# Two orders on VectorE in a gated attention and MLP kernel: A12 - S2 behind the forms of T2, and A22's scaling between two parts of A12's

## The chip, the cores and the metric

The kernel runs on one core of a Trainium2 chip. The metric is the device time of one execution in microseconds; 731.65 is the median of the three runs before the change. A core has a matrix engine (TensorE, PE in the profile), a vector engine (VectorE, DVE), an engine for activations and copies (ScalarE, ACT), GpSimd (POOL), and SyncE (SP), which here only issues transfers. Each engine has an instruction stream of its own and works it off in order; semaphores join them. The DMA engines move data between the core's memory and HBM.

## The reference

x is 2048 tokens by 1024. Two branches work on it and a gate per token mixes them:

```python
    x = A_x
    g = _sigmoid((x * gate_w).sum(-1, keepdims=True))
    a = _A_ref(x, A_wqkv, A_wo)
    b = _B_ref(x, B_w_gate, B_w_up, B_w_down)
    return g * a + (1 - g) * b
```

Branch A is attention with 32 heads of 32, in which a token sees 8 keys, itself and every second one before it (offsets 0, 2, ... 14); its output is multiplied by wo (1024 by 1024). Branch B is an MLP: h = gelu(x @ w_gate) * (x @ w_up) with 3584 columns, then h @ w_down. Both last products end in the same 2048 by 1024 result.

## The kernel before, in words

**Stages.** First come the projections (q, k, v, and 14 pairs of gate and up), with the attention worked off on DVE beside them. `h` and the attention's output are stored to HBM (`h_d`, `o_d`). Then comes the down stage. It treats both last products as one: the row of left operands is [h, attention output], the right operand is w_down above wo. It is done in two passes of 1024 tokens: `down(0)`, then `down(1)`.

**One pass.** The left operand is cut into four blocks A11, A12, A21, A22 (a half of the tokens by a half of the inner rows), the right one into R11, R12, R21, R22. The product is made with Winograd's form of Strassen's scheme: seven block products instead of eight, on sums of blocks. On the left these are S1 = A21 + A22 (`S` in the code), S3 = A11 - A21 (`AD`), S2 = A22 - S3 (written over A21), and S4 = A12 - S2 (written over A12). On the right they are T1 to T4, made earlier, stored in HBM and loaded back. The products are A11 R11, A12 R21, S1 T1, S2 T2, A12 R22 (where A12 holds S4 by then), S3 T3 and A22 T4. Three of them in pass 0, and four in pass 1, are cut once more in the same way (`level2`): that needs second-level sums, four for the left block (`forms_L`, line 985) and four for the right one (`forms_R`, line 993), all on DVE. `level2` is 126 matmuls of 256 columns (line 1024); a plain block product (`mm`, line 1049) is 72 matmuls of 512 columns.

**Scaling.** h has to be multiplied by 1 - g. For the last 2 of the 14 pairs that is done before h is stored. For the first 12 (`NE_` = 12) it is done in the loaded blocks, in place, by `scale_task` (line 906), four row groups to an instruction, so a block takes three. The sums of blocks (`comb_task`, line 913) take five instructions for a block of 18 row groups.

**Buffers.** Ten buffers of one block each hold everything, by the table `plan`. In pass 0 A12 is in buffer 2, A22 in 3, A21 in 6 and S in 8; R21 and then L6 (the left forms for S2) are in 7; T1 and then R6 (the right forms for T2) are in 1; T2 is in 9; A11, L5 and R22 follow each other in 4, and R11, R5 and T4 in 5. A load into a buffer waits until its last reader is done.

**The order around the change.** The order on each engine is that of the program text; nothing reorders it. Near the end of the projections `pre_down_2` issues the load of A22 (its first 12 row groups) and queues the scalings as tasks that run once the last projection is done. A12's and A21's first 11 row groups were loaded before; `pre_down_3` loads their twelfth, with R21 and the attention's rows, on SyncE's queue in this order: R21, A12's row and attention rows, A21's row and attention rows, A22's attention rows. The loads of T1 and T2 stand behind them. When the tasks are done, `down(0)` runs on DVE: the scaling of A21's last row group, S, AD, the forms of S and T1 (L5, R5), S2 over A21, the forms of S2 (L6), then the lines that the change touches, then `joins` (line 1013), which adds a part of the second-level product to the banks that ScalarE then copies out (line 1106). PE in the meantime runs A11 R11, A12 R21 and `level2` for S1 T1 and for S2 T2; the latter begins with two products that take S2 and T2 as they are, and its third product takes the first forms. In pass 1 (`last`) the lines of the change don't apply: there the five pieces of A12 - S2 stand behind the forms of T2.

```python
            run(forms_L(B["L6"], S2))
            rest = comb_task(A12, A12, S2, ALU.subtract)
            if not last:
                take(rest, 3)
            run(forms_R(B["R6"], B["T2"]), rest)
```

`take(rest, 3)` issues three of the five pieces of A12 - S2; `run` issues all that is left of its generators, one after the other.

Of the kernel before, what the change touches and what calls it, by code (L numbers as in the profile page):

```python
# [68 lines left out]
def kernel(  # L69
# [54 lines left out]
    NE_ = NPAIR - 2  # L124
# [10 lines left out]
    with tc.manual_schedule(engines={mybir.EngineType.PE, mybir.EngineType.DVE, mybir.EngineType.Activation,  # L135
# [296 lines left out]
        def bg(gen, prio, wake):  # L432
            t = Task(gen, prio, wake)
            tasks.append(t)
            tasks.sort(key=lambda t_: t_.prio)
            return t
# [288 lines left out]
        def pv_all():  # L725
# [48 lines left out]
            while now[0] < n - 6:  # L774
                yield None
            pre_down_2(0)

        def late_forms():
# [31 lines left out]
        def load_A(b, s, half, c, i0, i1, with_o, eng=nc.sync):  # L810
            for e, (a, z) in enumerate(((i0, min(i1, NE_)), (max(i0, NE_), i1))):
                if z > a:
                    src = h_d[s][e][:, :, c * SC:(c + 1) * SC].rearrange("p (i two) s -> p i two s", two=2)
                    eng.dma_start(out=b[:, a:z, :], in_=src[:, a - e * NE_:z - e * NE_, half, :])
            if with_o:
                nc.sync.dma_start(out=b[:, NH_:NK, :], in_=o_d[s][c][:, half * 4:half * 4 + 4, :])
# [81 lines left out]
        def Bs(s):  # L898
            return {k: bufs[v] for k, v in plan[s].items()}

        def scale_task(b, s, c, ia, ib):
            t0 = s * SUP + c * SC
            om = omgrep[:, t0:t0 + SC].rearrange("p (o s) -> p o s", o=1)
            for i0 in range(ia, ib, 4):
                i1 = min(i0 + 4, ib)
                TT(out=b[:, i0:i1, :], in0=b[:, i0:i1, :], in1=om.to_broadcast([P, i1 - i0, SC]), op=ALU.mult)
                yield 0.05 + 0.273 * (i1 - i0)

        def comb_task(o_, a, b, op, step=4):
            for i0 in range(0, NK, step):  # L910
                i1 = min(NK, i0 + step)
                f = lambda t_: flat(t_[:, i0:i1, :])
                TT(out=f(o_), in0=f(a), in1=f(b), op=op)  # L913
                yield 0.05 + 0.273 * (i1 - i0)

        def run(*gens):
            for g in gens:
                for _ in g:
                    pass
# [5 lines left out]
        def take(g, k):  # L925
            for _ in range(k):
                if next(g, None) is None:
                    break
# [14 lines left out]
        def pre_down_2(s):  # L943
            pd["end"] = True
            load_A(Bs(s)["A22"], s, 1, 1, 0, NE_, False)
            for k, c in (("A12", 0), ("A22", 1)):
                bg(scale_task(Bs(s)[k], s, c, 0, NE_), 7, n)
            if now[0] >= NX0 + 3:
                pre_down_3(s)

        def pre_down_3(s):
            loads(s, "R21")
            load_A(Bs(s)["A12"], s, 1, 0, KX, NE_, True)
            load_A(Bs(s)["A21"], s, 0, 1, KX, NE_, True)
            load_A(Bs(s)["A22"], s, 1, 1, 0, 0, True)
# [24 lines left out]
        def forms_L(f, b):  # L980
            f = quads(f)
            q = lambda kh, h: quarter(b, kh, h)
            for o_, a, b_, op in ((f[:, 0], q(0, 1), q(1, 1), ALU.add), (f[:, 1], f[:, 0], q(0, 0), ALU.subtract),
                                  (f[:, 2], q(0, 0), q(0, 1), ALU.subtract), (f[:, 3], q(1, 0), f[:, 1], ALU.subtract)):
                TT(out=o_, in0=a, in1=b_, op=op)  # L985
                yield 1.3

        def forms_R(f, b):
            f = quads(f)
            q = lambda kh, h: quarter(b, kh, h)  # L990
            for o_, a, b_, op in ((f[:, 0], q(0, 1), q(0, 0), ALU.subtract), (f[:, 1], q(1, 1), f[:, 0], ALU.subtract),
                                  (q(0, 1), q(1, 1), q(0, 1), ALU.subtract), (f[:, 2], q(1, 0), f[:, 1], ALU.subtract)):
                TT(out=o_, in0=a, in1=b_, op=op)  # L993
                yield 1.3

        def woven(*gens):
            for cs in zip(*gens):
                yield from cs
# [41 lines left out]
        def down(s):  # L1040
            B = Bs(s)
            last = s == 1
# [18 lines left out]
            A11, A12, A21, A22, S, AD = (B[k] for k in ("A11", "A12", "A21", "A22", "S", "AD"))  # L1061
            XP = [bank(XT[j]) for j in range(4)]
            VP = [bank(VT[j]) for j in range(4)]
            if last:
                run(scale_task(A12, s, 0, 0, NE_))
                level2(XT, A11, B["R11"], B["L1"], B["R1"])
                rest = comb_task(AD, A11, A21, ALU.subtract)
# [28 lines left out]
            level2(VT, S, B["T1"], B["L5"], B["R5"])  # L1096
            run(forms_L(B["L6"], S2))
            rest = comb_task(A12, A12, S2, ALU.subtract)
            if not last:
                take(rest, 3)  # L1100
            run(forms_R(B["R6"], B["T2"]), rest)

            def mid6():
# [13 lines left out]
            rest = woven(forms_L(B["L7"], AD), forms_R(B["R7"], B["T3"]))  # L1117
# [24 lines left out]
        n = len(units)  # L1142
# [4 lines left out]
        def run_last(b):  # L1147
            now[0] = b
            prv = units[b - 1]
            for t_ in [t_ for t_ in tasks if t_.wake < b]:  # L1150
                t_.finish()
            prv.p73()
            first = down(0)
            next(first)
            prv.p4()
            loads(0, "T1", "T2")
            for t_ in list(tasks):
                t_.finish()
            run(first)
            run(down(1))  # L1160
# [60 lines left out]
```

## Time and profile before

| | |
|---|---|
| median of 3 runs | 731.65 us (731.50 to 731.73) |
| the profiled execution | 731.21 us, span 729.4 us |
| PE busy | 714.7 us (98%), mean granted clock 0.995 |
| DVE busy | 655.1 us (90%) |
| ACT busy | 317.2 us (43%) |
| POOL busy | 114.7 us (16%) |
| PE matmuls of `level2` (line 1024) | 882, 100.3 us, mean 277 ns |
| PE matmuls of `mm` (line 1049) | 492, 109.3 us, mean 379 ns |
| DVE sums of blocks (line 913) | 40, 41.9 us, mean 1110 ns |
| pass 0 in the trace | from 512.5 us (first matmul of line 1049) to about 623 |
| pass 1 in the trace | from about 623 us to 729 |

How to read it: the span is the time from the first to the last instruction in the profile; the device time of that execution is 1.8 us longer. Matmuls overlap in the array, so the mean length of one is longer than the distance from one to the next. Engines carry line numbers of the kernel before; a line of the trace's timeline gives start, length, engine, line, operation, operands, how many instructions were merged into it, and in brackets how long the engine was idle before and what it waited for. A row of the windows gives the stretch, its length, the busy time with the number of instructions of PE, the weight loads, DVE, ACT and POOL, then the granted TensorE clock, the busy share of the DMA engines and the GB/s.

### The profile page before, as it was taken

What the parts mean: (1) busy time and instruction counts of PE and PEld (TensorE: products, weight loads), DVE (VectorE), ACT (ScalarE), POOL (GpSimd) and SP (SyncE); (2) the same over time, 40 slices, a digit from 0 to 9 for tenths busy, and PEclk for the clock granted to TensorE, in tenths of its full rate; (3) what the DMA queues carried; (4) which work ended last, traced back from release to release, by engine and by line L of the source; (5) the groups of instructions that cost most, each with busy time, mean ns of one, the idle gap of its engine ahead of it and who ended that gap; (6) DMA issues with size and microseconds to landing.
All of it is one profiled execution on the core that took longest, in us unless ns stands there. A gap on an engine that the chain in (4) does not pass through costs nothing. (4 is left out here: it accounts for less than half of the span.)

```text
span 729.4 us, 10330 instructions
## 1 busy us (share of the span) xinstructions
PE 714.7 (98%) x3883; PEld 393.0 (54%) x3945; DVE 655.1 (90%) x703; ACT 317.2 (43%) x570; POOL 114.7 (16%) x212
## 2 busy tenths in 40 slices
PE   8999999999999999999999999999998999999998
PEld 4466666655544444444444444444457666758573
DVE  3699999999999999999999999999599698799944
ACT  4554445444557665555555555555131211232210
POOL 1233445143201210000010000001110011110001
PEclk9999999999999999999999999999999899999999
DMA  9967644287274834443363836563975766965501
GB/s 279 279 184 224 206 140 154 78 283 268 98 213 136 284 118 146 137 154 113 120 203 115 276 118 224 133 234 100 364 315 179 271 229 211 380 276 199 199 22 58
DMA packets 112626, 140.78 MB, mean 193 GB/s; under 512 B 18832, under 2 KB 94768, under 8 KB 111552
## 3 DMA queue, kind: packets, MB, share of 16 engines
q1 hardware_dynamic: 98368, 98.38, 42.0%
q0 software_dynamic: 13920, 41.21, 15.7%
q8 instruction: 31, 0.51, 0.3%
q10 hardware_dynamic: 288, 0.52, 0.3%
q14 instruction: 19, 0.16, 0.1%
HBM read 98.01 MB, written 39.99 MB: 189 GB/s over the span
## 5 line engine op out<-in xcount | busy, mean ns | idle before, releaser
L364 PE MATMUL banks<-arena 128*128 128x512 bf16 x2136 | 472.1, 380 | 4.1 <-DVE arena L401 0.7
L364 PEld LDWEIGHTS <-arena 128*128 128x128 bf16 x2184 | 240.2, 111 | 235.6 <-issue 7.0
L1049 PE MATMUL banks<-arena 128*128 128x512 bf16 x492 | 109.3, 379 | 1.0 <-ACT arena L1106 0.4
L401 DVE TENSOR_TENSOR arena<-banks,arena 128x1024 bf16<-128x1024 f32 x78 | 95.2, 1220 | 13.0 <-PE banks L364 7.6
L1024 PE MATMUL banks<-arena 128*128 128x256 bf16 x882 | 100.3, 277 | 3.7 <-DVE arena L993 3.7
L387 ACT COPY arena<-banks 128x512 f32<-128x512 f32 x78 | 45.7, 586 | 130.8 <-PE banks L364 130.8
L1024 PEld LDWEIGHTS <-arena 128*128 128x128 bf16 x882 | 87.3, 99 | 16.8 <-issue 4.2
L1049 PEld LDWEIGHTS <-arena 128*128 128x128 bf16 x504 | 49.2, 98 | 59.1 <-issue 0.6
L372 ACT CAST arena<-banks 128x512 bf16<-128x512 f32 x102 | 59.6, 584 | 42.4 <-PE banks L364 42.4
L743 DVE TENSOR_TENSOR arena<-arena 128x2048 bf16<-128x2048 bf16 x64 | 77.0, 1219 | 0.5
L750 DVE TENSOR_TENSOR arena<-arena 128x2048 bf16<-128x2048 bf16 (+2 forms) x96 | 73.8, 775 | 1.0
L596 DVE TENSOR_TENSOR arena<-arena 128x2048 bf16<-128x2048 bf16 x64 | 74.6, 1218 | 0.1
L394 ACT COPY banks<-banks 128x512 f32<-128x512 f32 x78 | 44.5, 570 | 21.9 <-PE banks L364 20.1
L258 POOL DMA_DIRECT2D h_d<-arena x28 | 15.1, 541 | 242.0 <-DVE arena L252 213.1
L382 ACT COPY banks<-banks 128x512 f32<-128x512 f32 x78 | 45.0, 576 | 13.6 <-PE banks L364 12.1
L1054 POOL DMA_DIRECT2D out_dram<-arena x28 | 15.2, 541 | 179.8 <-DVE arena L1058 130.0
L913 DVE TENSOR_TENSOR arena<-arena 128x2048 bf16<-128x2048 bf16 (+1 forms) x40 | 41.9, 1110 | 0.0
L1029 ACT COPY banks<-banks 128x256 f32<-128x256 f32 x42 | 14.9, 356 | 57.2 <-PE banks L1024 57.0
L321 DVE TENSOR_TENSOR arena<-arena 128x1024 bf16<-128x1024 bf16 x60 | 38.6, 685 | 0.5
L252 DVE TENSOR_TENSOR arena<-arena 128x2048 bf16<-128x2048 bf16 x28 | 34.0, 1216 | 5.5 <-ACT arena L372 4.1
L370 ACT ACTIVATE arena<-banks 128x512 bf16<-128x512 f32 x54 | 32.2, 597 | 15.4 <-PE banks L364 15.4
L985 DVE TENSOR_TENSOR arena<-arena 128x2304 bf16<-128x2304 bf16 x28 | 37.5, 1352 | 0.5
(85 smaller groups left out, 434.1 us busy)
## 6 DMA issues: line engine op xcount, KB each, us to landing
arena<-t_d SPq DMA_DIRECT2D x8, 2304.0 KB, 12.5
h_d<-arena POOLq DMA_DIRECT2D x28, 512.0 KB, 3.6
arena<-in_B_w_down_dram SPq DMA_DIRECT2D x6, 1792.0 KB, 14.5
t_d<-arena POOLq DMA_DIRECT2D x36, 256.0 KB, 4.1
arena<-h_d SPq DMA_DIRECT2D x6, 1536.0 KB, 11.0
arena<-in_B_w_gate_dram SPq DMA_DIRECT2D x15, 512.0 KB, 5.2
arena<-in_B_w_up_dram SPq DMA_DIRECT2D x15, 512.0 KB, 4.6
arena<-in_B_w_down_dram SPq DMA_DIRECT2D x28, 256.0 KB, 7.0
```

The source lines that it names most:

```text
L364: self.pe = nc.tensor.matmul(ps, lhsT=self.L[form](kt), rhs=rhs[:, kt, :], start=(start and kt == 0), stop=(kt == HK - 1), skip_group_chec ...
L372: nc.scalar.copy(out=o_, in_=i_)
L382: nc.scalar.copy(out=self.Y, in_=self.X)
L387: nc.scalar.copy(out=self.p5s, in_=self.V)
L394: nc.scalar.copy(out=self.Z, in_=self.Y)
L401: TT(out=self.T[:, :, c2s], in0=pair, in1=self.p5s.rearrange("p (o n) -> p o n", o=1).to_broadcast([P, 2, SC]), op=ALU.add)
L596: TT(out=dst, in0=q.rearrange("p (o s) -> p o s", o=1).to_broadcast([P, NWIN, AC]), in1=_win_ap(k, [[-DIL, NWIN], [1, AC]]), op=ALU.mult)
L743: TT(out=prod2[(t // 2) % 2][:, t % 2], in0=ab, in1=_win_ap(v[:, t, HALO:HALO + AC], [[SJ, NJ], [-DIL, NWIN], [1, SJ]]), op=ALU.mult)
L750: TT(out=out_, in0=h(0), in1=h(1), op=ALU.add)
L913: TT(out=f(o_), in0=f(a), in1=f(b), op=op)
L1024: nc.tensor.matmul(c(i, h, j), lhsT=l[:, kt, j * P:(j + 1) * P], rhs=r[:, kt, :], start=False, stop=(kt == KH - 1), skip_group_check=True)
L1049: nc.tensor.matmul(ps, lhsT=L[:, i, j * P:(j + 1) * P], rhs=R[:, i, :], start=(start and q == 0), stop=(q == NK - 1), skip_group_check=not ...
```

## The change

Two edits. In `pre_down_2` the scaling of A12 is cut into two tasks, and A22's task is put between them: before, DVE scales A12's three pieces and then A22's three; after, A12's first two, A22's three, and then A12's third, which holds the twelfth row group. In `down`, pass 0 no longer issues three pieces of A12 - S2 ahead of the forms of T2: all five come behind them, as in pass 1.

```diff
         def pre_down_2(s):
             pd["end"] = True
             load_A(Bs(s)["A22"], s, 1, 1, 0, NE_, False)
-            for k, c in (("A12", 0), ("A22", 1)):
-                bg(scale_task(Bs(s)[k], s, c, 0, NE_), 7, n)
+            for k, c, ia, ib in (("A12", 0, 0, 8), ("A22", 1, 0, NE_), ("A12", 0, 8, NE_)):
+                bg(scale_task(Bs(s)[k], s, c, ia, ib), 7, n)
             if now[0] >= NX0 + 3:
                 pre_down_3(s)
...
             run(forms_L(B["L6"], S2))
             rest = comb_task(A12, A12, S2, ALU.subtract)
-            if not last:
-                take(rest, 3)
             run(forms_R(B["R6"], B["T2"]), rest)
```

## The prediction

> **What bounds the kernel now.** The page's first part comes first: TensorE (PE) is busy 98% of the span and VectorE (DVE) 90%, so only places where PE stands still can be worth time. The chain of waits goes back from the end to 656.13 us alone, too late for this change. So I took the list of waits, then PE's and DVE's timelines around its two rows:
>
> ```profile
> DVE arena L906 <- DMA arena<-h_d: 3.0, 1, 3.0
> PE banks L1024 <- DVE arena L993: 3.7, 1, 3.7
> ```
>
> (Columns: total us, times, longest.) DVE once waits 3.0 us for a load in the scaling; PE once waits 3.7 us for DVE's forms of T2. PE's timeline (start, length, instruction) around that wait, and two lines of the second pass:
>
> ```profile
> 544.42 18.00 PE L1024 MATMUL banks<-arena 128*128 128x256 bf16 x162
> 566.08 12.64 PE L1024 MATMUL banks<-arena 128*128 128x256 bf16 x90 [3.67 <-DVE arena L993]
> 578.56 15.70 PE L1049 MATMUL banks<-arena 128*128 128x512 bf16 x70
> ...
> 652.69 27.88 PE L1024 MATMUL banks<-arena 128*128 128x256 bf16 x252
> 680.95 15.70 PE L1049 MATMUL banks<-arena 128*128 128x512 bf16 x70 [0.39 <-ACT arena L1106]
> ```
>
> The same 252 matmuls (two level2 calls) take 34.14 us start to start in pass 0 (578.56 - 544.42) and 28.26 in pass 1. The wait is only 3.67 of it: 90 matmuls after it take 12.48 us, against 9.95 at pass 1's rate (27.88/252 = 110.6 ns). The windows give the reason in the column PEclk, TensorE's granted clock:
>
> ```profile
> 544.40:562.40 18.00, 18.00 (x163) 15.81 (x162) 17.80 (x16) 5.11 (x13) 0.54 (x1) 1.00 0.36 113
> 566.10:568.00 1.90, 1.90 (x10) 1.31 (x10) 1.86 (x2) 0.00 (x0) 0.00 (x0) 0.50 1.00 427
> 568.00:570.00 2.00, 2.00 (x11) 1.40 (x10) 2.00 (x3) 0.37 (x1) 0.00 (x0) 0.50 0.44 184
> 572.00:573.00 1.00, 1.00 (x12) 0.89 (x10) 0.98 (x2) 0.38 (x2) 0.00 (x0) 1.00 0.00 0
> 680.50:681.00 0.50, 0.12 (x2) 0.05 (x1) 0.50 (x2) 0.50 (x2) 0.00 (x0) 1.00 0.00 0
> ```
>
> The clock is half after the 3.67 us wait, full again by 572, and stays full over pass 1's 0.39 us stall. DVE up to the wait:
>
> ```profile
> 520.01 2.36 DVE L906 TENSOR_TENSOR arena<-arena,omgrep 128x2048 bf16<-128x2048 bf16 x2
> 525.37 4.97 DVE L906 TENSOR_TENSOR arena<-arena,omgrep 128x2048 bf16<-128x2048 bf16 x5 [3.00 <-DMA arena<-h_d]
> 530.25 10.37 DVE L913 TENSOR_TENSOR arena<-arena 128x2048 bf16<-128x2048 bf16 x10
> ...
> 556.00 5.36 DVE L985 TENSOR_TENSOR arena<-arena 128x2304 bf16<-128x2304 bf16 x4
> 561.27 3.49 DVE L913 TENSOR_TENSOR arena<-arena 128x2048 bf16<-128x2048 bf16 x3
> 564.68 5.35 DVE L993 TENSOR_TENSOR arena<-arena 128x2304 bf16<-128x2304 bf16 x4
> 569.95 1.82 DVE L913 TENSOR_TENSOR arena<-arena 128x2048 bf16<-128x2048 bf16 x2
> 571.69 1.29 DVE L1013 TENSOR_TENSOR banks<-banks,arena 128x512 f32<-128x512 f32 x2
> ```
>
> From 530.25 to 572.98 DVE has no idle time, and at 561.27, just before PE runs dry, it does three pieces of A12 - S2, which nobody needs before 578.56. Last, two loads on SyncE's queue (start, length of the issue):
>
> ```profile
> 504.63 0.53 SPq L814 DMA_DIRECT2D arena<-h_d  x1
> 516.96 0.47 SPq L814 DMA_DIRECT2D arena<-h_d  x1
> ```
>
> The first is A22's main load, 11.7 us to landing by the DMA view, so in place at 516.3. The second is A21's last row block, 11.6 us, in place at 528.56. A12's last block, issued at 513.90 with 11.4 us, lands at 525.3: DVE's wait above.
>
> **The change, part by part.** No instruction is added or removed; eleven DVE instructions trade places (four scalings, four forms, three pieces of A12 - S2). The queues of SP, ACT and POOL, and PE, keep their order.
>
> (1) A22's scaling into the 3.0 us wait. After A12's first two pieces DVE is free at 520.01 + 2 x 1.14 (pitch of this row) = 522.29. A22 landed at 516.3, so its three pieces run to 525.70 and A12's third to 526.84. PE's product with A12 begins about 528.5 (544.42 less 72 matmuls at 220.5 ns, from 27.79/126) and reads that third piece eight matmuls later: no wait, 3 us of cover. What is late next is A21's last block: the queued seventh L906 waits for 528.56, is done about 528.95, and the sums (L913) start there and not at 530.25. So DVE gains 1.3 us of the 3.0. Bounds: 0 (block later than 529.9) and 3.0. I take 1.3, by the landing. Behind it A22's attention rows (517.94 + 13.1 = 531.0) are wanted by the fourth sum at 528.95 + 3 x 1.04 = 532.1, and T1 (518.54 + 19.0 = 537.5) by the first form of T1 at 540.5: no new wait. The 1.3 us alone would shorten PE's wait from 3.67 to 2.4.
>
> (2) A12 - S2 behind the forms of T2. The first form starts when L985 ends: 561.27 - 1.3 = 559.97. It writes over T1's buffer, whose last reader on PE is matmul 126 from 544.42, at 558.4; T2 landed at 543.3. PE started 1.40 us after that form's start (566.08 - 564.68), so it could go on at 561.4; it wants to at 562.3. The wait is gone, with 1.0 us to spare. The next forms come every 1.27 us, the products that take them every 2 us. Without part (1) the sum is 562.67: 0.3 us of waiting. Clock: no stall, so full rate.
>
> (3) What is late next. Five pieces now stand between the forms and the joins (L1013), where two stood; DVE's total to that point is the same, so the joins start at 571.69 - 1.3 = 570.4. In pass 1 PE started 1.36 us after the joins did (680.95 - 679.59, one join and ACT's first copy L1106): 571.8 here. PE would be there at 544.42 + 27.87 = 572.3. Spare 0.5 us. This is the narrowest place: without part (1) it would cost 0.7.
>
> (4) Downstream. R22 has landed (556.55 + 7.8 = 564.4), and so has T3 (558.52 + 11.4 = 569.9). From 578.56 on every row hangs on PE or DVE, so it comes 6.3 us earlier, but T4's load (issued at 573.00, after the joins) only 1.2, and the next pass's A11 and R11 stand behind it. With 16 DMA engines full from 573 on, R11's last part, which landed at 597.3 (581.77 + 15.5), should land about 596.1; the form that needs it started at 604.88, now 598.6. Its first part, 595.6 before and 594.4 then, is wanted at 596.1. Hidden, by 1.7 us; and should the cover go, DVE has 5.4 us before PE notices (last zeroing by ACT ends 618.0, PE takes the banks at 623.39).
>
> Sum: 34.14 - 27.87 = 6.27 us, of which 3.74 is waiting and 2.53 the half clock. The profiled execution took 731.21 (span 729.4), so 724.9; the median of the runs shown is 731.65, 0.44 above it, so **725.4 us**. Something under 0.2% (1.5 us) this kernel's measurement could not tell from none.
>
> The clock's 2.53 us is the one term that a rule may contest. The Trainium skill, "TensorE: Matmul & The Clock Gate", Part 1, has the clock fall to half after one idle window of about 3.4 us, and says that the windows run free of the kernel. An estimate by that page: a 3.67 us wait holds a whole window in under one execution of ten, so most executions would not pay for the clock, and the gain would be 3.7 us.
>
> **The rivals.**
> - *The next wait is the joins (or A21's block comes late).* A lead of 0 leaves 0.74 us of stall: 731.65 - 5.53 = 726.1. For it: 0.5 us of room. Against: pass 1 has this very order and stalls 0.39 with DVE about 0.9 later against PE than here.
> - *The half clock is not in the timed runs, since its fall depends on when the wait begins.* Then 731.65 - 3.7 = 727.9. Against: the profiled time, with the fall in it, is 0.44 us below the median and the three runs lie within 0.23; a mix would spread by 2.5.
> - *The time is given back to loads.* R11 later than 601.5 (596.1 and the 5.4 of slack) costs PE; at 607.8 all is gone: 731.6. Against: that is 12 us beyond the estimate, with half of the DMA engines' time free from 590 to 600 (share 0.59).
> - *Slower.* A22 now stands before A12's third piece. Were A22 to land after 526 (530.7, when PE reads that piece, less 4.5 for four scalings), PE would wait us for us, and 4 us later for long enough to halve the clock again: landing at 530.5 costs 4.5 and 2.5, so 732.4 even with the gain. It landed at 516.3.
>
> **How the numbers follow.** Forecast 0.77; joins 0.09; no clock term 0.04; loads 0.04; slower 0.04; 0.02 is left for what I don't see, split between the last two signs. The likeliest case's own range is 724.9 to 726.0 (the runs' spread, and half of the spare places gone). The whole range goes down to 724.7 (pass 1's 0.39 stall gone too, and the spread), up to 727.4: the joins' case at 726.1 plus half of the clock's 2.53, because no row shows at what stall between 0.39 and 3.67 the clock falls. Faster 0.90, within 0.2% 0.05, slower 0.05.
>
> **What would show it.** In the profile of after: no row in which PE's L1024 waits for L993; 252 matmuls of L1024 in one line of about 27.9 us from 544.4; PEclk 1.00 from 560 to 580; L906 as five pieces without a gap, a wait of about 1.7 us ahead of the seventh, and the sums from about 529; the joins' start near 570.4; the end of the span near 723.1. Wrong would be: a stall ahead of L1049 at 572 (step 3), a load ahead of L906 or L993 between 590 and 600 (step 4), or the same shape at a gain of 3.7 (the clock).

## The result, and the profile after

The changed kernel takes 725.20 us (median of four executions, 724.93 to 725.62) against 731.69 before (731.50 to 732.37, four executions). The ratio is 0.991, with a 95% interval of 0.9893 to 0.9927. Later, against other executions of before, it took 725.12 us, ratio 0.9901 (0.9887 to 0.9916). The forecast was 725.4, and 724.9 to 726.0 for the likeliest case.

TensorE's timeline after, from the first block product of pass 0 on (start, length, instruction; in brackets the idle time before and what ended it; line 1104 is 1106 of the kernel before):

```profile
517.60 27.79 PE L1049 MATMUL banks<-arena 128*128 128x512 bf16 x128
545.22 27.83 PE L1024 MATMUL banks<-arena 128*128 128x256 bf16 x252
572.88 15.70 PE L1049 MATMUL banks<-arena 128*128 128x512 bf16 x72
...
647.01 27.87 PE L1024 MATMUL banks<-arena 128*128 128x256 bf16 x252
675.27 15.70 PE L1049 MATMUL banks<-arena 128*128 128x512 bf16 x72 [0.39 <-ACT arena L1104]
```

The two lines of 162 and 90 matmuls with a gap of 3.67 us between them have become one line of 252. From its start to the start of A12 R22 it is now 572.88 - 545.22 = 27.66 us; before it was 34.14. So this place gave 6.48 us between the two profiled executions. The span went down by only 5.6 (729.4 to 723.8), because the execution after reached the place 0.80 us later (545.22 against 544.42). Other profiled executions of kernels with this change reached it at 544.4 to 544.8, so that part is scatter ahead of the change.

The windows after, first for the stretch in which TensorE stood still before the change and then with bounds that are shown of before (PE, weight loads, DVE, ACT and POOL busy, granted TensorE clock, DMA share, GB/s):

```profile
562.40:566.10 3.70, 3.70 (x36) 3.33 (x34) 3.69 (x3) 0.75 (x2) 0.00 (x0) 1.00 1.16 422
566.10:568.00 1.90, 1.90 (x20) 1.69 (x19) 1.90 (x3) 0.71 (x2) 0.00 (x0) 1.00 1.02 437
568.00:570.00 2.00, 2.00 (x21) 1.79 (x19) 2.00 (x3) 0.71 (x2) 0.00 (x0) 1.00 0.79 331
```

The clock stays at 1.00, and TensorE does 21 matmuls in the window from 568 to 570, where it did 11 at half clock. VectorE after:

```profile
520.82 5.76 DVE L906 TENSOR_TENSOR arena<-arena,omgrep 128x2048 bf16<-128x2048 bf16 x5
528.05 1.23 DVE L906 TENSOR_TENSOR arena<-arena,omgrep 128x2048 bf16<-128x2048 bf16 x1 [1.48 <-DMA arena<-h_d]
529.59 0.43 DVE L906 TENSOR_TENSOR arena<-arena,omgrep 128x512 bf16<-128x512 bf16 x1 [0.31 <-DMA arena<-h_d]
529.93 10.37 DVE L913 TENSOR_TENSOR arena<-arena 128x2048 bf16<-128x2048 bf16 x10
...
555.68 5.36 DVE L985 TENSOR_TENSOR arena<-arena 128x2304 bf16<-128x2304 bf16 x4
560.95 5.35 DVE L993 TENSOR_TENSOR arena<-arena 128x2304 bf16<-128x2304 bf16 x4
566.22 5.22 DVE L913 TENSOR_TENSOR arena<-arena 128x2048 bf16<-128x2048 bf16 x5
571.36 2.49 DVE L1013 TENSOR_TENSOR banks<-banks,arena 128x512 f32<-128x512 f32 x4
```

Five scalings run without a gap, then VectorE waits twice: for A12's twelfth row (1.48 us) and for A21's (0.31). The forms of T2 (line 993) follow those of S2 at once. Measured against TensorE's start on S1 T1, the sums start at 529.93 - 545.22 = -15.29 us; before it was 530.25 - 544.42 = -14.17. So the lead is 1.12 us.

### The profile page after: what moved, and what is told of

The parts are those of the page before. It is cut to its first block, busy times and chain, and to the rows that moved or that the text cites. A ratio compares the mean times of both kernels' runs of the same rounds, so it can differ in the third digit from the quotient of the medians.

```text
span 723.8 us, 10393 instructions
## 1 busy us (share of the span) xinstructions
PE 716.1 (99%) x3945; PEld 392.7 (54%) x3945; DVE 654.7 (90%) x703; ACT 317.6 (44%) x570; POOL 115.1 (16%) x212
## 5 line engine op out<-in xcount | busy, mean ns | idle before, releaser
L1024 PE MATMUL banks<-arena 128*128 128x256 bf16 x882 | 97.5, 273 | 0.0
L258 POOL DMA_DIRECT2D h_d<-arena x28 | 15.2, 542 | 242.5 <-DVE arena L252 213.8
L382 ACT COPY banks<-banks 128x512 f32<-128x512 f32 x78 | 45.0, 576 | 13.6 <-PE banks L364 12.4
L1054 POOL DMA_DIRECT2D out_dram<-arena x28 | 15.2, 543 | 173.3 <-DVE arena L1058 123.5
```

What stands on the lines that cost most here:

```text
L382: nc.scalar.copy(out=self.Y, in_=self.X)
L1024: nc.tensor.matmul(c(i, h, j), lhsT=l[:, kt, j * P:(j + 1) * P], rhs=r[:, kt, :], start=False, stop=(kt == KH - 1), skip_group_check=True)
```

## The experiments

The theory to be tested was that of the prediction: the gain is TensorE's wait and the half clock behind it; the order of A12 - S2 takes most of it away; the scaling order gives VectorE a lead of about 1.1 us that keeps the next waits away; more lead is worth nothing. The rivals: the scaling order carries the gain, or is worth nothing; the clock term is not real, or falls by another rule than the one stall in the profile suggests.

### Each edit alone

The second edit alone, on the kernel before:

```diff
             rest = comb_task(A12, A12, S2, ALU.subtract)
-            if not last:
-                take(rest, 3)
             run(forms_R(B["R6"], B["T2"]), rest)
```

> Only the second edit (A12 - S2 behind the forms of T2); the scaling order is that of before. My theory: the 3.67 us wait and the half clock both go, but DVE lacks the 1.1 us lead that the after profile shows. PE then stalls about 0.3 us ahead of the third product of S2 T2 and about 0.7 us ahead of A12 R22, where it waits for the joins and the first copy: 725.2 + 1.0 = 726.2, no row with a clock under 1. Rival 'the scaling order carries the gain': 731 or more. Rival 'the scaling order is worth nothing': 725.2.

Measured: 726.90 us (726.54 to 727.27), ratio 0.9928 (0.9913 to 0.9943). TensorE's timeline in this run:

```profile
544.55 18.00 PE L1024 MATMUL banks<-arena 128*128 128x256 bf16 x162
563.52 9.99 PE L1024 MATMUL banks<-arena 128*128 128x256 bf16 x90 [0.97 <-DVE arena L993]
573.89 15.70 PE L1049 MATMUL banks<-arena 128*128 128x512 bf16 x70 [0.38 <-ACT arena L1104]
```

Both expected stalls are there, at the expected places and with a clock of 1.00. They sum to 1.35 us of idle time, where 1.0 was expected. From start to start the place takes 573.89 - 544.55 = 29.34 us, 1.68 more than the 27.66 of the kernel after, and the medians differ by as much (726.90 - 725.20 = 1.70). The expectation added two numbers of which the second contains the first: by the prediction a lead of 0 costs 0.74 in all. Most of the rest is that A12's row landed at 526.2 in this execution, so that the sums started 13.47 us ahead of S1 T1 instead of the 14.17 of the profile before. So the second edit alone stays 1.7 us above both edits together; against the executions of before that were taken with it (median 732.92) it brings 6.0 us. The scaling order is worth neither all nor nothing.

The first edit alone, on the kernel before:

```diff
-            for k, c in (("A12", 0), ("A22", 1)):
-                bg(scale_task(Bs(s)[k], s, c, 0, NE_), 7, n)
+            for k, c, ia, ib in (("A12", 0, 0, 8), ("A22", 1, 0, NE_), ("A12", 0, 8, NE_)):
+                bg(scale_task(Bs(s)[k], s, c, ia, ib), 7, n)
```

> Only the first edit (A22's scaling between A12's parts); three pieces of A12 - S2 stay ahead of the forms. PE's wait should shrink from 3.7 to about 2.6 us. If any wait of this length halves the clock afterwards: 731.7 - 1.1 = 730.6, with rows of clock 0.50 behind the wait. If the clock falls only after a wait of about 3.4 us or more (the Trainium skill, 'TensorE: Matmul & The Clock Gate', Part 1): no such row, 725.2 + 2.6 = 727.8. If the loss is in proportion to the wait: 729.6.

Measured: 729.46 us, ratio 0.9959 (0.9944 to 0.9973). The executions don't agree: four lie between 729.35 and 729.95 with a mean granted clock of 0.997 or 0.998, the fifth is 727.88 with 0.999. In the profiled one, which is one of the four, TensorE waits 2.67 us, from about 562.8 to 565.42. Its windows:

```profile
565.00:566.00 1.00, 0.58 (x6) 0.52 (x6) 0.90 (x2) 0.00 (x0) 0.00 (x0) 1.00 0.69 295
566.00:567.00 1.00, 1.00 (x9) 0.77 (x7) 1.00 (x2) 0.22 (x1) 0.00 (x0) 0.65 1.38 590
568.00:569.00 1.00, 1.00 (x6) 0.72 (x5) 1.00 (x2) 0.29 (x1) 0.00 (x0) 0.50 1.25 535
569.00:570.00 1.00, 1.00 (x8) 0.72 (x6) 1.00 (x2) 0.08 (x1) 0.00 (x0) 0.64 0.14 55
```

And two windows of the profile before:

```profile
564.00:565.00 1.00, 0.00 (x0) 0.00 (x0) 1.00 (x2) 0.00 (x0) 0.00 (x0) 0.86 0.69 295
571.00:572.00 1.00, 1.00 (x8) 0.78 (x7) 1.00 (x3) 0.12 (x1) 0.00 (x0) 0.73 0.06 16
```

In shorter windows of these traces the clock is 1.00 or 0.50, except in the one in which it changes, so a mean in between tells when it changed. The reader sees the clock fall at 566.3, when TensorE had been at work again for almost 1 us, and rise at 569.7: half clock for 3.4 us. In the profile before it fell at about 564.7, within the wait, and rose at 571.5: 6.8 us, twice as long. So neither "any such wait costs 2.5" nor "no loss under 3.4 us of wait" holds; the loss comes in stretches. The third rival, a loss in proportion to the wait, has its number here (729.6 expected, 729.46 measured), but it falls with the next run: there a wait of 1.52 us costs no clock at all. The execution at 727.88 is where the kernel would be without a stretch (727.8 was expected); that its clock did not fall is read from its mean of 0.999 only, as it has no profile.

### More and less waiting

Two and five pieces of A12 - S2 ahead of the forms, on the kernel after (which has none there):

```diff
             rest = comb_task(A12, A12, S2, ALU.subtract)
+            if not last:
+                take(rest, 2)
             run(forms_R(B["R6"], B["T2"]), rest)
```

> The kernel after, but with two of the five pieces of A12 - S2 ahead of the forms of T2 (before: three, after: none). The forms start 2.1 us later than in the kernel after, which had 0.8 us to spare, so PE waits about 1.4 us. Clock kept: 725.2 + 1.4 = 726.6. Clock halved as before: 729.1.

Measured: 726.42 us (726.23 to 726.78). Two lines of its timeline:

```profile
564.08 9.98 PE L1024 MATMUL banks<-arena 128*128 128x256 bf16 x90 [1.52 <-DVE arena L993]
573.90 15.70 PE L1049 MATMUL banks<-arena 128*128 128x512 bf16 x70
```

The wait is 1.52 us, the 90 matmuls behind it run at full rate (573.90 - 564.08 = 9.82 us from start to start), and all four executions have a mean clock of 1.0. A wait of this length cost itself and nothing more.

With `take(rest, 5)` in the same place:

> The kernel after, but with all five pieces of A12 - S2 ahead of the forms of T2. PE waits about 4.4 us (5.2 us of pieces less 0.8 us of room). If the wait halves the clock for about 5.5 us behind it, as before: 725.2 + 4.4 + 2.5 = 732.1, slower than the kernel before. If the clock term were not real: 729.6. If the loss grows with the wait beyond it: 733.

Measured: 731.84 us over ten executions (731.17 to 732.36), ratio 0.9988 (0.9979 to 0.9998). TensorE:

```profile
567.07 12.79 PE L1024 MATMUL banks<-arena 128*128 128x256 bf16 x90 [4.41 <-DVE arena L993]
579.69 15.70 PE L1049 MATMUL banks<-arena 128*128 128x512 bf16 x70
```

The wait is the 4.4 us worked out. The 90 matmuls take 12.62 us from start to start, 2.80 more than the 9.82 of the run before this one. In the profile before, the loss was 2.66 (12.48 - 9.82) behind a wait of 3.67 us, and with the first edit alone 1.67 (576.91 - 565.42 less 9.82) behind 2.67. So a wait 0.7 us longer adds 0.14 us to the loss. The loss is, to within 0.1 us, half of the time that TensorE works at half clock, from its restart, or the fall of the clock where that comes later, to the rise: here 567.07 to 572.8 (a mean of 0.58 in the window from 572 to 573), which is 5.8 us; 5.5 in the profile before; 3.4 with the first edit alone. What of the low clock lies within the wait costs nothing.

The median is within 0.3 us of the 732.1 worked out. But it is not slower than the kernel before, as was expected: the executions of before that were taken with it have a median of 732.92. That kernel has the old scaling order, and its wait can be longer than the 3.67 us of its profile, as the next run suggests; its slower executions have no profile, so this isn't shown.

One piece, with the scaling order of before, to put the wait between 1.52 and 2.67:

```diff
             if not last:
-                take(rest, 3)
+                take(rest, 1)
```

> The kernel before with its scaling order, and one piece of A12 - S2 ahead of the forms of T2 where it had three. PE's wait should be that of the run with the second edit alone (0.97 us) and one piece (1.14): 2.1 us, between the 1.52 that left the clock alone and the 2.67 that halved it in four executions of five. Clock kept: 727.2 to 727.4. Clock halved for one stretch of 3.4 us behind the wait: 728.9 to 729.1. A mix of both, by execution, if what decides is where the wait lies against a window that runs free of the kernel.

Measured: 729.38 us, but six executions from 727.86 to 731.51, by mean clock 0.999, 1.0, 0.998 (three) and 0.995. The profiled one is the slowest. VectorE and TensorE there:

```profile
527.58 4.97 DVE L906 TENSOR_TENSOR arena<-arena,omgrep 128x2048 bf16<-128x2048 bf16 x5 [4.81 <-DMA arena<-h_d]
```

```profile
566.03 12.88 PE L1024 MATMUL banks<-arena 128*128 128x256 bf16 x90 [3.21 <-DVE arena L993]
```

The wait was 3.21 us and not 2.1: A12's row landed at 527.58, 2.2 us later than in the profile before (1.8 later against the start of S1 T1). So with the old scaling order the wait itself changes by up to 1.8 us between profiled executions with the landing of one 128 KB row, and the clock's loss comes on top: two stretches in the profiled execution (0.58 in the window from 565 to 566, 0.50 from 571 to 572, 1.00 from 572 on), and by the means alone none or one in the others. The run shows the mix by execution, and does not place the length at which the clock begins to fall.

### What the lead is worth, and the narrowest place

The twelfth rows of A12 and A21 loaded first, on the kernel after (`load_A(..., 0, 0, True)` loads the attention's rows alone):

```diff
         def pre_down_3(s):
+            load_A(Bs(s)["A12"], s, 1, 0, KX, NE_, False)
+            load_A(Bs(s)["A21"], s, 0, 1, KX, NE_, False)
             loads(s, "R21")
-            load_A(Bs(s)["A12"], s, 1, 0, KX, NE_, True)
-            load_A(Bs(s)["A21"], s, 0, 1, KX, NE_, True)
+            load_A(Bs(s)["A12"], s, 1, 0, 0, 0, True)
+            load_A(Bs(s)["A21"], s, 0, 1, 0, 0, True)
```

> The kernel after, with the twelfth rows of A12 and A21 loaded ahead of R21 and the attention's rows instead of behind and between them. If A21's row is what cut DVE's gain from 3.0 to 1.1 us (step 1), DVE's waits of 1.48 and 0.31 us in the scaling go and the sums start about 1.8 us earlier against PE. In time that is worth nothing if PE has no wait left for DVE in pass 0: 725.2, same. Rival: R21 lands later and PE waits for it at the start of A12 R21: slower by what R21 is late, 0.6 us or more.

Measured: 724.97 us (724.80 to 725.56); the kernel after, in its two sets, 725.20 and 725.12. VectorE in this run:

```profile
520.09 7.23 DVE L906 TENSOR_TENSOR arena<-arena,omgrep 128x2048 bf16<-128x2048 bf16 x7
527.24 3.49 DVE L913 TENSOR_TENSOR arena<-arena 128x2048 bf16<-128x2048 bf16 x3
531.33 6.97 DVE L913 TENSOR_TENSOR arena<-arena 128x2048 bf16<-128x2048 bf16 x7 [0.60 <-DMA arena<-o_d]
```

All seven scalings now run without a gap, so the two rows were what cut the lead; the run moves both, and doesn't part A12's from A21's. The attention's rows are late next (0.60 us). The sums start 17.25 us ahead of S1 T1 (544.49 - 527.24) instead of 15.29. In time nothing moved that this measurement can tell: TensorE had no wait left for it. The rival falls too: R21, now behind the two rows, is not waited for (the line of A11 R11 and A12 R21 takes 544.49 - 516.86 = 27.63 us up to S1 T1, and 545.22 - 517.60 = 27.62 in the kernel after).

The joins of S1 T1 ahead of the pieces of A12 - S2, in both passes, on the kernel after:

```diff
-            run(forms_R(B["R6"], B["T2"]), rest)
+            run(forms_R(B["R6"], B["T2"]))
+            joins(VT, B["R5"])
+            run(rest)
 
             def mid6():
-                joins(VT, B["R5"])
                 for j in range(4):
```

> The kernel after, with the joins of S1 T1 put right behind the forms of T2, ahead of the five pieces of A12 - S2, in both passes. My theory (step 3 of the prediction: the joins are the narrowest place, and pass 1's 0.39 us stall is theirs): the stall ahead of A12 R22 in pass 1 goes, T4's load in pass 0 starts about 5 us earlier, nothing else moves: 725.2 - 0.4 = 724.8, and PE is at 100% from the first product of pass 0 to the end. Rival: the pieces of A12 - S2, now 1.3 us later, become what A12 R22 waits for, and nothing is won: 725.2 or a little more.

Measured: 724.39 us (724.24 to 725.03), ratio 0.989 (0.9874 to 0.9906). Pass 1 in this run:

```profile
646.53 27.88 PE L1024 MATMUL banks<-arena 128*128 128x256 bf16 x252
674.25 15.70 PE L1049 MATMUL banks<-arena 128*128 128x512 bf16 x70
```

The stall of 0.39 us is gone, and the pieces, now behind the joins, did not become a wait. From the start of `level2` to the start of A12 R22 it is 27.72 us, and 28.26 in the kernel after (675.27 - 647.01): 0.54 less. The median lies 0.8 us below the kernel after's, where 0.4 was expected; the two were taken apart, and what the remainder is stays open. Both edits together, beside the kernel after on the same chip:

> The kernel after once more, on the same chip and against the same runs of before as the next one, so that the two can be set side by side: 725.2.

> Both small edits on the kernel after: the joins ahead of A12 - S2, and the twelfth rows of A12 and A21 loaded first. The joins take pass 1's 0.39 us away; the rows are worth nothing in time: 0.4 us under the kernel after, 724.8. Rival: the two stalls were hiding a load behind them, so that nothing or more than 0.4 moves.

Measured: the kernel after 725.12 us (724.93 to 725.49), both edits on it 724.26 (724.19 to 725.17). The profiles of the two (725.15 and 724.19 us) say what is the edit's: pass 1 from the start of `level2` to the start of A12 R22 takes 28.27 us in the first (646.62 to 674.89) and 27.72 in the second (646.20 to 673.92), 0.55 less. The other 0.4 stands ahead of both edited places: A22's load, which is issued before the rows, starts at 505.05 and 504.63, and the first `level2` at 544.83 and 544.41. It is of the size of the scatter there. This is the fastest version, by an amount that its profile shows and its times, whose ranges overlap, don't establish by themselves.

## Why the prediction was right

*Step 1, A22 into the wait.* Right in its size, and only in part in what came late: the lead came out at 1.12 us for the 1.3 worked out, and A21's row was the last to be waited for (0.31 us), but ahead of it VectorE waited 1.48 us for A12's own row, which the step had in place in time. The step took one landing for the rule: A12's row landed at 525.37 in the profile before, at 526.2 and 527.58 in two other runs with the old order, and between 526.5 and 528.05 in the runs with the new one. With the old order every such delay goes straight to the sums, which start 14.2, 13.5 or 12.4 us ahead of S1 T1; with the new one it is behind A22's pieces, and the six profiled runs that have it with the old loads start 15.2 to 15.3 ahead. Over these profiles the new order adds 1.9 us of lead on average and not 1.1, and it steadies the lead. That it steadies the time isn't shown: the second edit alone spreads by 0.73 us, the kernel after by 0.69.

*Step 2, the forms of T2 at once.* Right: line 993 starts behind line 985 without a wait for T1's buffer, and TensorE runs on. The room was 0.8 us instead of 1.0 (the form's start at 560.95, plus the 1.40 us that it takes to TensorE, against 545.22 + 17.9 = 563.1). Without the first edit the step has 0.3 us of waiting there; the run has 0.97, with a lead 0.7 us shorter than that of the profile before.

*Step 3, the joins as the narrowest place.* Right: ScalarE's first copy was done 0.2 us before TensorE wanted the bank (0.5 worked out), and without the first edit the stall appears just there. It also shows in pass 1, where moving the joins removes it.

*Step 4, loads downstream.* Right to the half microsecond: R11's two parts landed at 594.6 and 595.9 (579.92 + 14.7 and 580.90 + 15.0), 594.4 and 596.1 were worked out, and VectorE has no wait for a load between 585 and 605.

*The sum.* 6.27 us forecast for this place, 6.48 in the trace; at the medians 6.5 (731.69 to 725.20). That the gain agrees so closely is in part luck: the later sets of before have medians of 732.03, 732.40 and 732.92, and beside the one of 732.40 the kernel after (725.12) gains 7.3. The time of the kernel after was the steadier thing to forecast, since no wait of TensorE for VectorE is left in pass 0. The term that was mis-sized by the 0.2 is the undisturbed length of the 252 matmuls: pass 1's busy length of 27.87 was taken, but the next line starts before that line's modelled end, and from start to start it is 27.66.

*The clock.* The term was real, and the rival that left it out (727.9) fell. But the reason given against that rival, that a mixture would spread the times by 2.5 us, was weak: it rested on four executions. Over 14 executions taken later the kernel before lies between 731.31 and 733.75 us, with mean clocks from 0.994 to 0.998, so the term does differ from one execution to the next. Going by those mean clocks it is one stretch of half clock or two, not all or none: half clock for 3.4 of 730 us makes a mean of 0.998, for 6.8 us 0.995. Only the executions with a profile show it directly.

## What to carry to other kernels

On an in-order engine that feeds the bottleneck, put what is wanted first first, and let work that nobody waits for fill in behind it, also where a wait ahead of it seems to invite filling. Work that is ready goes ahead of work whose load may be late, which protects against the spread of landings as well as the mean. A stall of TensorE is priced with the matmuls behind it: start to start over the stage against the same matmuls in an undisturbed pass gave 6.5 us where the list of waits said 3.7.

## What the runs showed of the hardware that was not expected

The granted clock fell in stretches of about 3.4 us: one behind a wait of 2.67 us, two (6.8 us) behind the waits of 3.21, 3.67 and 4.41, none behind 1.52, 0.97 and 0.39. One stretch cost 1.7 us, two cost 2.7 to 2.9 (2.66 and 2.80, and 2.90 with one piece, where A12 R22 starts at 578.75: 578.75 - 566.03 - 9.82). The fall came 2.3 to 3.5 us after TensorE stopped, in one run after it had started again. The Trainium skill, "TensorE: Matmul & The Clock Gate", Part 1, has windows of about 3.4 us that run free of the kernel; stretches of that length and of twice it, and executions of one kernel with different losses, agree with it. Its condition, a whole idle window before the clock falls, does not: 2.67 us of wait were enough in the profiled execution, and by the mean clocks in three others of five.

How much of a window must be idle can be narrowed by an estimate from the traces. Lay windows of 3.41 us (half of the 6.8) so that one ends where the clock falls. In that window TensorE stood idle for 2.30 us in the profile before, and for 2.53, 2.35 and 3.35 in the runs with waits of 2.67, 3.21 and 4.41; the wait of 1.52 brought no fall (a mean clock of 1.0 in all four executions of that run). In the next window it was still idle for 1.36, 0.86 and 1.06 us in the three runs whose clock stayed low for a second stretch, and not at all in the one whose clock came back after the first. So two thirds of a window (2.30 of 3.41 us) were enough for a fall, and a quarter (0.86) was enough to keep the clock low. That is a reading of four falls, not an experiment, and a wait of one length can lie in the windows in different ways.
